# An attention and two-MLP kernel: SyncE's queue in the hand-written opening order, and preparations in nine steps

## The chip, the cores and the metric

The kernel runs on one NeuronCore of a Trainium2 chip. The metric is the device time of one execution in microseconds (us), as a median of several executions.

## The reference, cut to what matters

Chunked attention (chunks of 64 rows, 8 heads) feeds an MLP with squared ReLU, which feeds a gated MLP. Everything is float32.

```python
scores = scale * q_c @ k_c.T            # q, k, v: 8 x 8 x 576 x 64, chunks of 64
attn = exp(scores - max); attn /= sum(attn)
x = (attn @ v_c) as 4608 x 512
x = relu(x @ w_in) ** 2 @ w_out         # w_in 512 x 2048
out = (silu(x @ w_gate) * (x @ w_val)) @ w_out2
```

## The kernel before, in words

The 4608 tokens are nine blocks of 512. A block is two units of 256 tokens; attention works by units, numbered 0 to 17. The matrix products work by sets: set 0 is block 0 alone, sets 1 to 4 are pairs of blocks. A pair is multiplied with a seven-product scheme over the two blocks and the two halves of the contraction, a single block with four products. Each float32 product is three TensorE matmuls over a high and a low part (`three`, lines 517 to 522), so one of the seven products of a weight tile is six matmuls of 128x512.

The phases run one after another: the opening (attention of units 0 to 9, preparation of the eight weight tiles of w_in, the products of sets 0 and 1 with them), then w_in for sets 2 to 4 with the attention of the later units beside it, then `down1` (w_out, block by block), then w_gate and w_val, then w_out2.

**The opening** (lines 863 to 914) is a string of step names. Each name is a letter code and one digit, and the string is executed from left to right while the program is traced; PE, ACT, DVE and POOL execute their instructions in that order (`ordered`, line 916). SyncE (SP) was not in that list: the framework's own scheduler decided when each of its DMA issues goes into SyncE's queue. A queue executes in order, so an issue that waits holds up those behind it. The codes, with their lines:

- Attention of unit u: `qk` loads q and k (364), `v` loads v (369), `s` 64 small score matmuls (380), `m` the row maximum on DVE (397), `b` subtracts it on DVE (403), `e` exponential on ACT (406), `u` row sums and reciprocal on DVE (412 to 415), `w` the normalisation on POOL (419). Units 0 to 5 turn the rows with PE (`t`, 438) and copy them out on ACT (`c`, 450). Units 6 to 9 turn them on DVE (`zt`, 457), copy the square blocks on ACT (`zc`, 467) and then move four 32-row pieces per unit with DMAs of 64 KB on SyncE (line 471, tile p<-z). `y` is 64 small matmuls with v (495), `o` copies the result into x on ACT (511).
- Preparation of weight tile k: `raw` loads two tiles (115), `d1` on ACT (130, 131), `d2` on DVE (135, 136), `i` on POOL (143), `j` on DVE (148), `q` four sums on DVE (240 to 243), `h` and `g` the high parts on ACT (158), `l` and `n` the low parts on DVE (161), `st` stores the tile to DRAM on SyncE (256). `ld` loads a stored tile again (266).
- Operands of a set: `xd`, `xs`, `ys` differences on DVE (551), `xh`, `ph`, `qh` high parts on ACT, `xl`, `pl`, `ql` low parts on DVE, for sets 0, 1 and 2.
- Products of set 0 with tile k: `S` and `R` (twelve matmuls each), evicted by `sa` and `sb` on ACT. Products of set 1: `A`, `E`, `B`, `C`, `F`, `D`, `J` (six matmuls each), with the copies `ra`, `ub`, `vf` and the evictions `cd`, `cs` on ACT (610, 727, 736) and `ca`, `cb`, `cj` on DVE (596). Finished tiles g are stored by ACT's queue (737).

Three pools matter. Tiles of 128x1024 share 31 slots (`big`), the W tiles share 5, and the PSUM has six single banks plus one double bank. The double bank takes the scores and, from unit 6 on, the result of `y`. A load whose slot is not free waits in SyncE's queue for the release.

**Down1.** `beside_down1` (1189 to 1204) advances the preparation of the twelve tiles of w_gate and w_val by two steps after each of the products (b, i), from b = 1 on; `Prep.steps` (258 to 262) cuts one preparation into seven steps. When the last preparation has allocated its W tile, the first three stored W tiles are loaded (`up2.begin`, line 1201, `ahead` 3).

Of the kernel before, what the change touches and what calls it, by code (L numbers as in the profile page):

```python
# [29 lines left out]
def attention_mlp_mlp_kernel(  # L30
# [29 lines left out]
    nc = tc.nc  # L60
# [136 lines left out]
    class Prep:  # L197
# [58 lines left out]
                nc.sync.dma_start(out=wdram[self.key], in_=flat(self.w))  # L256

        def steps(self):
            for group in ("raw", "d1", "d2 i", "j h", "q", "g", "l n st"):
                for step in group.split():  # L260
                    getattr(self, step)()
                yield
# [8 lines left out]
    n2 = nf2 // 2  # L271
# [59 lines left out]
    class Work:  # L331
# [5 lines left out]
        def add(self, steps):  # L337
            self.queue.append(steps)
# [16 lines left out]
    at, vs = {}, {}  # L355
# [97 lines left out]
    def attn_z(u):  # L453

        e, pt = at[u], duo("p")
        z = duo("z")
        nc.vector.transpose(
            out=z.rearrange("p y (g t) -> p g y t", t=SQ),
            in_=e.rearrange("p j (g y t) -> p (j g) y t", y=2, t=SQ),
        )  # L460
        at[u] = z, pt

    def attn_squares(u):

        z, pt = at[u]
        at[u] = pt
        nc.scalar.copy(out=pt, in_=z)
        for c in range(2):
            for x in range(2):
                src, dst = c * CH + x * SQ, c * CH + (1 - x) * SQ  # L470
                nc.sync.dma_start(out=pt[dst:dst + SQ, x, :], in_=z[src:src + SQ, 1 - x, :])

    def attn_turn(u):
        attn_z(u)
        attn_squares(u)

    def attn_values(u):
        pt, vt = at.pop(u), vs.pop(u)
        if u < EARLY:
            xps = [bank("xps0"), bank("xps1")]  # L480
        else:
            xps = banks2("xps")
            xps = [xps[:, c, :] for c in range(2)]
        at[u] = xps
        for a in range(pairs):
            for n in range(2):
                for c in range(2):
                    for j in range(2):
                        h, g = 2 * a + j, (j * 2 + n) * pairs + a
                        part = slice(c * CH, (c + 1) * CH)  # L490
                        if u < EARLY:
                            rhs = pt[part, j ^ c, (n * pairs + a) * CH:(n * pairs + a + 1) * CH]
                        else:
                            rhs = pt[part, :, g * SQ:(g + 1) * SQ]
                        nc.tensor.matmul(
                            out=xps[c][j * CH:(j + 1) * CH, (a * 2 + n) * CH:(a * 2 + n + 1) * CH],
                            lhsT=vt[part, n, h * CH:(h + 1) * CH],
                            rhs=rhs,
                            start=True,
                            stop=True,  # L500
                        )
# [280 lines left out]
    n1 = nf1 // 2  # L782

    keys1 = [("i", fp) for fp in range(n1)]
# [8 lines left out]
    def ordered(*engines):  # L793

        return tc.manual_schedule(engines=set(engines))

    ET = mybir.EngineType
# [56 lines left out]
    up1 = Products(keys1, moving1, 2, 2, lambda key: Squared)  # L854

    def x_of(n):
        up1.ops[n] = Operands(xraw, sets[n])
        return up1.ops[n]

    def x_sums(n):  # L860
        x_of(n).sums()

    OPENING = """
        qk0 s0 raw0 d10 qk1 m0 b0 raw1 d20 i0 e0 qk2 s1 m1 d11 u0 v3 b1 j0 s2 qk3 e1 u1 m2 w0 raw2
        t0 w1 b2 h0 v1 d21 s3 t1 v0 q0 i1 c0 qk4 e2 y0 qk5 m3 u2 d12 b3 c1 s4 d22 w2 y1 m4 e3 t2 b4
        o0 v4 i2 u3 o1 e4 s5 c2 v2 w3 u4 m5 w4 xh1 y2 b5 xh2 t3 e5 c3 raw3 o2 xl2 t4 y3 c4 g0 u5 w5
        o3 l0 ph1 xl1 n0 t5 xd4 y4 v5 xh4 S0 j1 c5 raw4 y5 xl4 o4 qk6 h1 q1 pl1 g1 R0 o5 l1 n1 xs5
        sa0 sb0 xs6 xs7 ph6 ph2 A0 ra0 S1 pl6 R1 B0 pl2 ph7 ph5 j2 ub0 h2 pl7 q2 sa1 C0 s6 pl5 F0 l2
        d13 xs4 g2 n2 d23 A1 E0 ra1 B1 d14 sb1 ph4 S2 ca0 i3 C1 sa2 R2 j3 vf0 pl4 ph3 ub1 D0 cb0 sb2
        q3 pl3 h3 F1 st1 vf1 d24 raw5 l3 E1 A2 g3 n3 D1 ca1 i4 cb1 j4 ra2 cd0 B2 cd1 m6 J0 q4 C2 J1  # L870
        ub2 d15 cj1 d25 F2 g4 cj0 cs0 S3 A3 E2 ra3 sa3 h4 n4 i5 cs1 raw6 j5 vf2 B3 R3 ca2 cb2 ub3 C3
        d16 J2 F3 q5 l4 E3 d26 sb3 i6 D2 j6 h5 A4 vf3 cd2 ra4 ca3 D3 g5 B4 cb3 h6 ub4 J3 cj2 cs2 C4
        q6 raw7 g6 n5 l5 n6 b6 E4 ca4 cj3 cd3 F4 S4 d17 d27 vf4 A5 sa4 R4 D4 qk7 e6 ra5 i7 B5 j7 cb4
        l6 sb4 ub5 s7 C5 cs3 m7 st4 J4 F5 cd4 b7 u6 E5 A6 qk8 e7 ra6 q7 u7 qk9 s8 g7 cj4 B6 cs4 w7
        S5 m8 C6 n7 b8 h7 ca5 s9 sa5 ub6 w6 zt6 zc6 vf5 m9 l7 e8 zt7 zc7 F6 vf6 cb5 u8 R5 A7 v6 v7
        J5 b9 w8 ra7 cj5 B7 y6 S6 zt8 e9 o6 zc8 y7 sa6 o7 v8 st5 u9 D5 E6 y8 v9 cd5 w9 zt9 zc9 R6
        ca6 ub7 o8 sb5 C7 y9 S7 sb6 F7 R7 cb6 ca7 o9 J6 ys5 cs5 ys6 qh5 ys4 E7 sa7 D6 ys7 qh6 qh1
        ql1 sb7 ql5 vf7 cb7 st7 st2 ql6 qh2 cd6 qh7 qh4 ql2 ql4 ql7 qh3 cj6 ql3 ld1 cs6
    """

    def opening():

        jobs = {}

        def operands(n):
            return up1.ops[n] if n in up1.ops else x_of(n)

        def job(k, n=1):
            if (n, k) not in jobs:
                kind, late = ((Single, ()), (Pair, (1,)))[n]  # L890
                jobs[n, k] = kind(combos[keys1[k]], up1.ops[n], Squared(sets[n], k, late))
                jobs[n, k].use = (n, keys1[k])
            return jobs[n, k]

        steps = {
            "qk": attn_qk, "v": attn_v, "s": attn_products, "m": attn_max, "b": attn_less, "e": attn_exp,
            "u": attn_sums, "w": attn_normed, "t": attn_turn_pe, "c": attn_turned, "y": attn_values, "o": attn_out,
            "zt": attn_z, "zc": attn_squares, "ld": lambda m: up1.ask(up1.place[2, keys1[m]]),
        }
        for step in ("raw", "d1", "d2", "i", "j", "h", "q", "l", "g", "n", "st"):  # L900
            steps[step] = lambda k, step=step: getattr(preps[k], step)()
        for n, names in enumerate((("xd", "xh", "xl"), ("xs", "ph", "pl"), ("ys", "qh", "ql"))):
            for name, what in zip(names, ("sum", "high", "low")):
                steps[name] = lambda i, n=n, what=what: getattr(operands(n), what)(i)
        for name, what, i in (("S", "tile", 0), ("sa", "out", 0), ("R", "tile", 1), ("sb", "out", 1)):
            steps[name] = lambda k, what=what, i=i: getattr(job(k, 0), what)(i)
        parts = "A m1 ra k1 E m5 B m6 ub k6 C m2 ca k2 F m7 vf k7 cb o7 D m4 cd o4 J m3 cj o3".split()
        for name, what in zip(parts[::2], parts[1::2]):
            steps[name] = lambda k, what=what: getattr(job(k), what)()
        steps["cs"] = lambda k: job(k).take.square(1)  # L910
        for step in OPENING.split():
            steps[step[:-1]](int(step[-1]))
        jobs[1, n1 - 1].take.late = ()
        return jobs[1, n1 - 1]

    with ordered(ET.PE, ET.Activation, ET.DVE, ET.Pool):
        make_identity(nc, ident)
        up1.prev = opening()

# [187 lines left out]
    def attention_step(n, t):  # L1107

        if n < len(sets):
            units = [b * upb + x for b in sets[n] for x in range(upb)]  # L1110
            for what in ("out", "turn", "scores", "qk"):
                for u, when in zip(units, WHEN[what]):
                    if when == t:
                        if what == "out":
                            attn_values(u)
                            attn_out(u)
                        elif what == "turn":
                            attn_v(u)
                            attn_turn(u)
                        elif what == "scores":  # L1120
                            attn_scores(u)
                        else:
                            attn_qk(u)
# [193 lines left out]
```

## Time and profile before

| | us |
|---|---|
| median of 3 runs | 1645.68 |
| lowest, highest | 1643.70, 1648.36 |
| the profiled execution | 1643.45 |
| its span, first to last instruction | 1641.7 |
| PE busy | 1597.1 |

The profiled execution's own time is 1.75 us more than its span. PE is the tensor engine's matmul queue, PEld its weight loads, DVE the vector engine, ACT the scalar engine, POOL the GpSimd engine, SP SyncE; a q after a name is that engine's issue queue. A matmul's length in a row overlaps with its neighbours' (they are pipelined), so matmuls are counted by the distance of their starts. A bracket at the end of a row is the engine's idle time before it and what ended it; "issue" there means that the profile shows no releaser.

### The profile page before, as it was taken

Reading aid. Unit: us, or ns where it says so; the run is one execution under the profiler, and the core shown is the slowest. Engines: PE = TensorE matmul, PEld = TensorE weight load, DVE = VectorE, ACT = ScalarE, POOL = GpSimd, SP = SyncE. Lnnn points to the kernel's source line nnn. Section 1 sums busy time; section 2 is a strip of 40 time slices with the busy share of each in tenths; the row PEclk is TensorE's granted clock in tenths of the full one; section 3 lists DMA queues with packets and bytes.
Section 4 is the critical chain, followed back from the end, with each engine's and each line's share of the span. In section 5 each row is a group of like instructions: output and inputs, shape, how many; then the busy total and the mean of one; then the engine's idle time right before and its main releaser. Section 6 shows DMA issues by size and latency. Waiting matters only on the chain.

```text
span 1641.7 us, 23545 instructions
## 1 busy us (share of the span) xinstructions
PE 1597.1 (97%) x9408; PEld 1316.8 (80%) x9408; DVE 1017.7 (62%) x1248; ACT 760.5 (46%) x1069; POOL 150.4 (9%) x118
## 2 busy tenths in 40 slices
PE   5998999999999999999999999999999999999998
PEld 4787778888888888878888888888887787888886
DVE  7987465654487655553303556547458895887894
ACT  5875656666664443333211434334336553434441
POOL 4122030201131111100000000000000210000000
PEclk9999999999999999999999999999999999999999
DMA  8467697879767766774329676577668999564342
GB/s 321 181 250 245 227 338 266 295 252 341 265 229 256 267 246 256 256 285 157 116 67 388 217 282 230 194 256 244 216 246 299 366 393 408 211 205 132 101 140 52
DMA packets 136575, 397.92 MB, mean 242 GB/s; under 512 B 47760, under 2 KB 56976, under 8 KB 125584
## 3 DMA queue, kind: packets, MB, share of 16 engines
q1 hardware_dynamic: 118416, 345.02, 59.2%
q10 hardware_dynamic: 14592, 38.80, 6.3%
q0 software_dynamic: 3456, 12.58, 2.4%
q8 instruction: 74, 1.21, 0.3%
q14 instruction: 37, 0.30, 0.1%
HBM read 269.75 MB, written 123.47 MB: 240 GB/s over the span
## 4 chain that ended last, share of the span: by engine, by line
PE 52%; issue 6%; DMA 4%; DVE 2%; POOL 1%; SPq 0%; ACT 0%; POOLq 0%; DVEq 0%; ACTq 0%
PE px L520 8%; PE px L521 8%; PE px L522 8%; PE pz L520 4%; PE pz L521 4%; PE pz L522 4%; PE py L520 4%; PE py L521 4%; PE py L522 4%; DMA graw<-g 2%; PE acc L520 2%; PE acc L521 2%; PE acc L522 2%; DMA raw<-in_w_out_dram 1%; POOL m L143 1%
## 5 line engine op out<-in xcount | busy, mean ns | idle before, releaser
L520 PE MATMUL px<-hi,W 128*128 128x512 f32 x640 | 251.3, 393 | 1.9 <-ACT u L610 1.9
L521 PE MATMUL px<-hi,W 128*128 128x512 f32 x640 | 249.4, 390 | 0.0
L522 PE MATMUL px<-lo,W 128*128 128x512 f32 x640 | 249.4, 390 | 0.0
L143 POOL TENSOR_TENSOR m<-m,raw 128x512 int32<-128x512 int32 x68 | 97.2, 1446 | 1013.0 <-ACT r L610 552.5
L610 ACT COPY u<-px 128x512 f32<-128x512 f32 x160 | 92.6, 579 | 156.0 <-PE px L522 154.1
L520 PE MATMUL acc<-hi,w 128*128 128x512 f32 x416 | 162.3, 390 | 0.0
L521 PE MATMUL acc<-hi,w 128*128 128x512 f32 x416 | 162.1, 390 | 0.0
L522 PE MATMUL acc<-lo,w 128*128 128x512 f32 x416 | 161.6, 389 | 0.0
L161 DVE TENSOR_TENSOR lo<-graw,hi 128x1024 fp32r<-128x1024 f32 x72 | 92.2, 1281 | 83.8 <-ACT hi L158 51.1
L520 PEld LDWEIGHTS px<-hi,W 128*128 128x128 f32 x640 | 120.2, 188 | 29.9 <-ACT u L610 3.4
L158 ACT CAST hi<-h 128x1024 fp32r<-128x1024 f32 x93 | 95.6, 1053 | 96.5 <-PE py L521 16.3
L522 PEld LDWEIGHTS px<-lo,W 128*128 128x128 f32 x640 | 120.2, 188 | 25.0
L757 DVE TENSOR_TENSOR g<-g,sig 128x1024 f32<-128x1024 f32 x54 | 65.9, 1221 | 119.2 <-ACT sig L756 119.2
L521 PEld LDWEIGHTS px<-hi,W 128*128 128x128 f32 x640 | 120.2, 188 | 24.2
L520 PE MATMUL py<-hi,W 128*128 128x512 f32 x320 | 127.4, 398 | 0.4 <-DMA W<-wv 0.4
L520 PE MATMUL pz<-hi,W 128*128 128x512 f32 x320 | 124.9, 390 | 1.4 <-DVE g L593 1.4
L521 PE MATMUL py<-hi,W 128*128 128x512 f32 x320 | 125.7, 393 | 0.0
L522 PE MATMUL py<-lo,W 128*128 128x512 f32 x320 | 125.5, 392 | 0.0
L521 PE MATMUL pz<-hi,W 128*128 128x512 f32 x320 | 124.7, 390 | 0.0
L522 PE MATMUL pz<-lo,W 128*128 128x512 f32 x320 | 124.6, 389 | 0.0
L158 ACT CAST hi<-graw 128x1024 fp32r<-128x1024 f32 x72 | 75.5, 1049 | 88.7 <-DVE lo L161 36.7
L161 DVE TENSOR_TENSOR lo<-h,hi 128x1024 fp32r<-128x1024 f32 x93 | 110.2, 1212 | 4.5 <-issue 2.2
(125 smaller groups left out, 3055.1 us busy)
## 6 DMA issues: line engine op xcount, KB each, us to landing
W<-wv SPq DMA_DIRECT2D x30, 1792.0 KB, 9.0
g<-g ACTq DMA_DIRECT2D x72, 512.0 KB, 5.5
graw<-g SPq DMA_DIRECT2D x72, 512.0 KB, 4.4
W<-wg SPq DMA_DIRECT2D x20, 1792.0 KB, 8.3
h<-g SPq DMA_DIRECT2D x54, 512.0 KB, 8.2
h<-h SPq DMA_DIRECT2D x54, 512.0 KB, 6.2
W<-wi SPq DMA_DIRECT2D x15, 1792.0 KB, 10.0
raw<-in_w_out_dram SPq DMA_DIRECT2D x28, 512.0 KB, 8.2
```

Of the source, the lines that this page charges most:

```text
L143: nc.gpsimd.tensor_tensor(out=mi[:, t, :], in0=mi[:, t, :], in1=word(raw, 0, I32), op=ALU.add)
L158: nc.scalar.copy(out=hi, in_=src)
L161: nc.vector.tensor_tensor(out=lo, in0=src, in1=hi, op=ALU.subtract)
L520: nc.tensor.matmul(out=ps, lhsT=lh, rhs=rh, start=first, stop=False, skip_group_check=on)
L521: nc.tensor.matmul(out=ps, lhsT=ll, rhs=rh, start=False, stop=False, skip_group_check=on)
L522: nc.tensor.matmul(out=ps, lhsT=lh, rhs=rl, start=False, stop=last, skip_group_check=on)
L610: nc.scalar.copy(out=r, in_=self.x)
L757: nc.vector.tensor_tensor(out=g[j], in0=g[j], in1=s, op=ALU.mult)
```

## The change

SP joins the engines whose order is written out, until the end of the first pair. The moves of a unit's normed rows become a step of their own, `zd`, which the string places apart from `zc`. The string itself is another one: the same 396 steps and the four `zd`, in another order on every engine. One preparation of `Prep.steps` has nine steps in place of seven.

```diff
--- before.py
+++ after.py
@@ -256,7 +256,7 @@
                 nc.sync.dma_start(out=wdram[self.key], in_=flat(self.w))
 
         def steps(self):
-            for group in ("raw", "d1", "d2 i", "j h", "q", "g", "l n st"):
+            for group in ("raw", "d1", "d2 i", "j", "h", "q", "g", "l", "n st"):
                 for step in group.split():
                     getattr(self, step)()
                 yield
@@ -463,8 +463,12 @@
     def attn_squares(u):
 
         z, pt = at[u]
+        nc.scalar.copy(out=pt, in_=z)
+
+    def attn_moves(u):
+
+        z, pt = at[u]
         at[u] = pt
-        nc.scalar.copy(out=pt, in_=z)
         for c in range(2):
             for x in range(2):
                 src, dst = c * CH + x * SQ, c * CH + (1 - x) * SQ
@@ -473,6 +477,7 @@
     def attn_turn(u):
         attn_z(u)
         attn_squares(u)
+        attn_moves(u)
 
     def attn_values(u):
         pt, vt = at.pop(u), vs.pop(u)
@@ -861,21 +866,21 @@
         x_of(n).sums()
 
     OPENING = """
-        qk0 s0 raw0 d10 qk1 m0 b0 raw1 d20 i0 e0 qk2 s1 m1 d11 u0 v3 b1 j0 s2 qk3 e1 u1 m2 w0 raw2
-        t0 w1 b2 h0 v1 d21 s3 t1 v0 q0 i1 c0 qk4 e2 y0 qk5 m3 u2 d12 b3 c1 s4 d22 w2 y1 m4 e3 t2 b4
-        o0 v4 i2 u3 o1 e4 s5 c2 v2 w3 u4 m5 w4 xh1 y2 b5 xh2 t3 e5 c3 raw3 o2 xl2 t4 y3 c4 g0 u5 w5
-        o3 l0 ph1 xl1 n0 t5 xd4 y4 v5 xh4 S0 j1 c5 raw4 y5 xl4 o4 qk6 h1 q1 pl1 g1 R0 o5 l1 n1 xs5
-        sa0 sb0 xs6 xs7 ph6 ph2 A0 ra0 S1 pl6 R1 B0 pl2 ph7 ph5 j2 ub0 h2 pl7 q2 sa1 C0 s6 pl5 F0 l2
-        d13 xs4 g2 n2 d23 A1 E0 ra1 B1 d14 sb1 ph4 S2 ca0 i3 C1 sa2 R2 j3 vf0 pl4 ph3 ub1 D0 cb0 sb2
-        q3 pl3 h3 F1 st1 vf1 d24 raw5 l3 E1 A2 g3 n3 D1 ca1 i4 cb1 j4 ra2 cd0 B2 cd1 m6 J0 q4 C2 J1
-        ub2 d15 cj1 d25 F2 g4 cj0 cs0 S3 A3 E2 ra3 sa3 h4 n4 i5 cs1 raw6 j5 vf2 B3 R3 ca2 cb2 ub3 C3
-        d16 J2 F3 q5 l4 E3 d26 sb3 i6 D2 j6 h5 A4 vf3 cd2 ra4 ca3 D3 g5 B4 cb3 h6 ub4 J3 cj2 cs2 C4
-        q6 raw7 g6 n5 l5 n6 b6 E4 ca4 cj3 cd3 F4 S4 d17 d27 vf4 A5 sa4 R4 D4 qk7 e6 ra5 i7 B5 j7 cb4
-        l6 sb4 ub5 s7 C5 cs3 m7 st4 J4 F5 cd4 b7 u6 E5 A6 qk8 e7 ra6 q7 u7 qk9 s8 g7 cj4 B6 cs4 w7
-        S5 m8 C6 n7 b8 h7 ca5 s9 sa5 ub6 w6 zt6 zc6 vf5 m9 l7 e8 zt7 zc7 F6 vf6 cb5 u8 R5 A7 v6 v7
-        J5 b9 w8 ra7 cj5 B7 y6 S6 zt8 e9 o6 zc8 y7 sa6 o7 v8 st5 u9 D5 E6 y8 v9 cd5 w9 zt9 zc9 R6
-        ca6 ub7 o8 sb5 C7 y9 S7 sb6 F7 R7 cb6 ca7 o9 J6 ys5 cs5 ys6 qh5 ys4 E7 sa7 D6 ys7 qh6 qh1
-        ql1 sb7 ql5 vf7 cb7 st7 st2 ql6 qh2 cd6 qh7 qh4 ql2 ql4 ql7 qh3 cj6 ql3 ld1 cs6
+        qk0 s0 m0 raw0 d10 b0 qk1 e0 s1 d20 v1 u0 qk2 raw1 i0 m1 j0 b1 qk3 e1 v0 q0 w0 u1 w1 s2 m2
+        b2 qk4 d11 h0 raw2 d21 e2 u2 qk5 t0 s3 c0 t1 m3 b3 i1 v2 j1 y0 s4 g0 c1 y1 e3 w2 v3 o0 u3 m4
+        t2 w3 d12 b4 e4 c2 s5 d22 u4 i2 m5 o1 xh1 b5 xh2 e5 w4 xl2 v5 u5 t3 h1 w5 xl1 c3 y2 v4 t4 y3
+        c4 o2 o3 n0 l0 xd4 y4 t5 ph1 pl1 o4 S0 raw3 c5 A0 raw4 xh4 y5 q1 xl4 g1 d13 n1 ph2 l1 j2 q2
+        o5 h2 R0 S1 g2 st1 R1 ra0 sa0 sb0 l2 n2 xs5 xs6 S2 sa1 ph6 xs7 R2 sb1 pl6 pl2 ph7 B0 pl7 C0
+        ph5 pl5 qk6 ub0 sa2 F0 d23 A1 ca0 vf0 E0 cb0 ra1 B1 sb2 C1 ub1 i3 F1 xs4 ph3 j3 ph4 vf1 pl3
+        pl4 st2 A2 ca1 ra2 d14 h3 s6 E1 B2 q3 D0 J0 cb1 J1 raw5 g3 C2 d24 D1 l3 cd0 ub2 d15 cd1 n3
+        F2 cj1 raw6 cj0 A3 i4 j4 ra3 d25 vf2 cs0 q4 E2 h4 cs1 B3 g4 ub3 C3 D2 m6 E3 ca2 F3 d16 i5 S3
+        l4 j5 n4 qk7 ca3 d26 h5 vf3 cb2 cb3 i6 cd2 R3 j6 b6 sa3 J2 h6 sb3 J3 cj2 s7 A4 ra4 q5 st4 D3
+        B4 g5 S4 l5 raw7 e6 E4 q6 n5 cj3 l6 cs2 cd3 qk8 cs3 ub4 u6 g6 w6 C4 F4 n6 m7 A5 b7 ra5 qk9
+        d17 sa4 R4 e7 s8 ca4 d27 vf4 B5 zt6 C5 D4 zc6 ub5 u7 i7 sb4 S5 m8 j7 F5 A6 b8 cb4 zd6 sa5 w7
+        e8 ra6 s9 zt7 vf5 J4 D5 m9 cd4 v6 h7 v7 B6 q7 l7 R5 C6 zc7 zd7 ub6 cj4 b9 g7 n7 u8 v9 e9 u9
+        F6 A7 v8 sb5 E5 y6 w8 w9 ra7 ca5 B7 vf6 cb5 cd5 zt8 C7 zc8 o6 ub7 zt9 zc9 zd8 E6 J5 zd9 y7
+        o7 cj5 cs4 S6 y8 ca7 ca6 F7 o8 cb6 D6 y9 o9 st7 R6 ys5 cd6 ys6 ys7 J6 S7 sa6 ys4 E7 vf7 sb6
+        qh1 st5 qh5 qh2 ql1 ql5 sa7 qh6 R7 ql2 cb7 qh7 ql6 cj6 qh3 cs5 ql7 ql3 cs6 qh4 ql4 sb7 ld1
     """
 
     def opening():
@@ -895,7 +900,8 @@
         steps = {
             "qk": attn_qk, "v": attn_v, "s": attn_products, "m": attn_max, "b": attn_less, "e": attn_exp,
             "u": attn_sums, "w": attn_normed, "t": attn_turn_pe, "c": attn_turned, "y": attn_values, "o": attn_out,
-            "zt": attn_z, "zc": attn_squares, "ld": lambda m: up1.ask(up1.place[2, keys1[m]]),
+            "zt": attn_z, "zc": attn_squares, "zd": attn_moves,
+            "ld": lambda m: up1.ask(up1.place[2, keys1[m]]),
         }
         for step in ("raw", "d1", "d2", "i", "j", "h", "q", "l", "g", "n", "st"):
             steps[step] = lambda k, step=step: getattr(preps[k], step)()
@@ -913,7 +919,7 @@
         jobs[1, n1 - 1].take.late = ()
         return jobs[1, n1 - 1]
 
-    with ordered(ET.PE, ET.Activation, ET.DVE, ET.Pool):
+    with ordered(ET.PE, ET.Activation, ET.DVE, ET.Pool, ET.SP):
         make_identity(nc, ident)
         up1.prev = opening()
```

## Rows read from the trace of the kernel before

**Rows 1.** The page, part 1: busy time by engine, share of the span, instructions

```profile
PE 1597.1 (97%) x9408; PEld 1316.8 (80%) x9408; DVE 1017.7 (62%) x1248; ACT 760.5 (46%) x1069; POOL 150.4 (9%) x118
```

**Rows 2.** Stretches: length, busy time of PE, PEld, DVE, ACT, POOL, granted clock, DMA share, GB/s

```profile
0.00:53.00 53.00, 30.08 (x1090) 28.44 (x1091) 42.64 (x49) 30.07 (x52) 20.95 (x20) 0.94 0.81 294
53.00:156.00 103.00, 102.95 (x745) 84.09 (x743) 88.72 (x115) 74.90 (x109) 20.25 (x13) 1.00 0.61 228
156.00:186.00 30.00, 21.68 (x310) 17.47 (x309) 7.49 (x10) 13.61 (x28) 1.90 (x1) 0.83 0.68 231
```

**Rows 3.** Timeline of PE, 152 to 185 us: start, length, line, tile, count [idle before]

```profile
152.02 0.39 PE L520 MATMUL px<-hi,W 128*128 128x512 f32 x1
...
155.88 0.39 PE L522 MATMUL px<-lo,W 128*128 128x512 f32 x1
161.13 2.10 PE L495 MATMUL xps<-p,v 64*64 64x64 f32 x64 [4.86 <-issue]
163.15 0.79 PE L520 MATMUL py<-hi,W 128*128 128x512 f32 x1
...
167.99 1.16 PE L495 MATMUL xps<-p,v 64*64 64x64 f32 x64
...
181.11 2.22 PE L495 MATMUL xps<-p,v 64*64 64x64 f32 x64 [3.45 <-DMA p<-z]
...
184.53 0.39 PE L520 MATMUL py<-hi,W 128*128 128x512 f32 x1
```

**Rows 4.** Timeline of SyncE's queue, 152 to 178 us: issues, first start and length

```profile
152.75 1.44 SPq L369 DMA_DIRECT2D v<-in_v_dram  x2
154.24 13.59 SPq L471 DMA_DIRECT2D p<-z  x8
167.93 1.07 SPq L369 DMA_DIRECT2D v<-in_v_dram  x2
...
173.98 3.48 SPq L471 DMA_DIRECT2D p<-z  x4
```

**Rows 5.** Issue to landing: tile p, 140 to 190 us; tile v, until 190 us

```profile
DMA to landing us min/median/max: 1.9/3.7/8.8
...
DMA to landing us min/median/max: 3.9/10.0/12.1
```

**Rows 6.** Timeline of DVE and ACT, 154 to 174 us

```profile
154.94 0.69 DVE L596 CUSTOM_DVE_ANT_0 g<-pz,u 128x512 f32<-128x512 f32 x1 [0.47 <-PE pz L522]
...
163.26 1.20 ACT L511 COPY x<-xps 128x256 f32<-128x256 f32 x4 [7.63 <-PE xps L495]
163.32 1.25 DVE L457 STREAM_TRANSPOSE z<-e 128x1024 f32<-128x1024 f32 x1 [4.93 <-DMA p<-z]
...
172.91 1.05 ACT L467 COPY p<-z 128x1024 f32<-128x1024 f32 x1 [0.47 <-DVE g L596]
```

**Rows 7.** Timeline of all engines, 13 to 53 us

```profile
13.21 1.22 DVE L397 TENSOR_REDUCE mx<-s 128x16 f32<-128x1024 f32 x1 [1.44 <-PE s L380]
...
46.22 2.34 POOL L419 TENSOR_TENSOR e<-e,rec 128x1024 f32<-128x1024 f32 x1 [3.35 <-DVE rec L415]
46.72 2.92 DVE L161 TENSOR_TENSOR lo<-x,hi 128x1024 fp32r<-128x1024 f32 x1
...
51.83 1.28 DVE L148 SCALAR_TENSOR_TENSOR m<-raw,m 128x512 int32<-128x512 int32 x2
...
52.47 0.50 PE L520 MATMUL py<-hi,W 128*128 128x512 f32 x1
```

**Rows 8.** Waits of SyncE's queue, 60 to 120 us: total, times, longest

```profile
SPq L115 <- DMA g<-g: 7.2, 2, 6.6
```

**Rows 9.** The longest wait of PE after 300 us, and its stretch

```profile
PE accs L520 <- ACT hi L158: 2.0, 1, 2.0
...
730.00:740.00 10.00, 7.80 (x28) 5.50 (x27) 3.71 (x4) 4.21 (x4) 0.00 (x0) 0.83 0.79 288
```

**Rows 10.** Timeline of SyncE's queue, 706 to 725 us: one of three such issues

```profile
711.59 0.42 SPq L266 DMA_DIRECT2D W<-wv  x1
```

## The prediction

> **What bounds the kernel now.** Start with the page's busy times. TensorE (PE) is busy for 1597.1 us [rows 1] of a span of 1641.7, so no order of any queue can win more than the 44.6 us in which PE stands idle, plus what its slow clock costs. The next view is the table of stretches, which shows where those idle times lie. In the first 53 us PE is busy for 30.1, so 22.9 are idle, while DVE works for 42.6. From 53 to 156 us PE is never short of work, and from 156 to 186 it is idle for 8.3 us again, at a granted clock of 0.83 on average [rows 2]. After 300 us its longest single wait is 2.0 us [rows 9]. The change touches the two idle places and nothing between 186 and 440.
>
> The timeline of PE shows what the second place is. The last of the products ends at 156.1 us (a start at 155.88 and one matmul). PE then waits 4.86 us for `y6`, and 3.45 us ahead of `y9` [rows 3]. After each wait the records show matmuls at the lower clock level, 1.2 GHz, until work had run for some us. SyncE's queue says why. v6 and v7 were issued only at 152.75, eight moves then occupy the queue until 167.8, v8 and v9 follow at 167.93, and the moves of unit 9 at 173.98 [rows 4]. A v load takes 10.0 us to land in the median, a move 3.7 [rows 5]. So `y6` waited for SyncE (v6 or the moves of unit 6, the row names neither), and `y9` for the moves of unit 9, which waited for ACT's `zc9` at 172.91 [rows 6].
>
> **The change, part by part.**
>
> The second idle place. A matmul's pitch is (155.88 - 152.02) / 17 = 0.227 us, so a product of six takes 1.36 us and one of twelve (`S`, `R`) 2.72; a `y` at the full clock takes 1.16 [rows 3]. What can go is 4.86 + 3.45 = 8.31 us of idle time, and the slow stretches behind it. From 161.13 these are 2.10 - 1.16 = 0.94 for `y6` and (167.99 - 163.15) - 12 x 0.227 = 2.12 for the twelve matmuls after it. From 181.11 they are 184.53 - 181.11 - 1.16 - 3 x 0.227 = 1.58 [rows 3]. Together it is 12.95 us.
>
> Does the new order remove it? It puts J4 D5 B6 R5 C6 F6 A7 E5 between `s9` and `y6`, which is 7 x 1.36 + 2.72 = 12.2 us of work, where the old one had F6 R5 A7 J5 B7, 8.2 us. v6 follows `zd6` in SyncE's queue. Counting tiles against the 31 slots, it needs at the latest the slots of q9 and k9, which `s9` frees. So even from there it has 12.2 us against a landing of 10.0 in the median and 12.1 at most [rows 5], and `y6` is met. `zd6` needs `zc6`, which the string has some 20 us of PE work ahead of `y6`.
>
> The later units run closer. Up to `y6` the new order holds one product fewer than the old one had up to 156.1. With the first product `S0` at 51.2 (below), `y6` starts at 51.2 + (156.1 - 52.5) - 1.36 = 153.5. Then B7 C7 E6 J5 put `y7` at 160.1, S6 puts `y8` at 164.0, F7 and D6 put `y9` at 167.9. Against this stands unit 8: E5 ends at 153.5, `cb5` takes 0.69, `zt8` 1.25, `zc8` 1.05 [rows 6], so `zd8` can start at 156.5. Its last of four issues starts some 2.6 later (3.48 for four [rows 4]) and lands 3.7 after that, at 162.8; with the longest landing of 8.8 [rows 5], at 167.9. So `y8` has 1.2 us to spare, or is 3.9 late. For unit 9 ACT does `o6` (1.20 [rows 6]) and one half-size copy (about 0.6, half of `zc`) ahead of `zc9`, which is done by 159.4; the last move starts at 162.6 and lands at 166.3, or 171.4. `y9` has 1.6 to spare, or is 3.5 late, unless a late `y8` has moved it too. The worst is therefore 3.9 and a slow stretch as that behind `y9` now, 1.6: 5.5 us. I take half, 2.75, since both margins are small against the spread of the landings. The operands of set 2 follow `y9` by about 8 us, and 10.9 us of products (R6 J6 S7 E7 R7) stand ahead of their first use, so nothing new is late there.
>
> The first idle place. The new string sends the loads up to k1 in the old order, so the first score products stay where they are. On DVE, `u0` now stands ahead of `m1` and fills the 1.44 us in which DVE waited for the second score product; `j1` comes ahead of the last sums `u5` and adds 1.28. On PE, `y4` moves ahead of `t5`, which waits for POOL's normalisation until 48.6 (46.22 + 2.34), so `S0` no longer stands behind `y4`: 1.16 less [rows 3, 7]. The sum is -1.3, which puts `S0` at 51.2 in place of 52.47. That `n0` now stands ahead of `l0` costs nothing as long as `xl1`, `n0`, `l0` on DVE (three instructions of 1.2 us or less, or 5.0 with `xl1` at the 2.92 it took beside POOL [rows 7]) stay within the 2.34 of the normalisation and the two to three us of `t5`, which come out near the same. Bounds: 3 us less, or 3 more if DVE is slowed beside POOL as `xl1` was.
>
> The middle, 53 to 156 us. SyncE's issues are now fixed: `st1` ahead of qk6, `st2` ahead of raw5, raw7 ahead of qk8. Each store waits for DVE's `n`, and every load behind it waits with it; behind raw7 stand `s8` and `s9`. By counting, DVE's parts are ready ahead of PE throughout, nearest at `B0` (2.9 us), and the six banks never bind. The slots are nearly all taken at raw5 and raw6. Nothing hides a late slot fully: the longest wait of that kind is 6.6 us, a raw load that waited for ACT's store of g [rows 8]. I take 0, since qk7, raw7 and qk8 have two or more slots to spare, and keep 0 to 6.6.
>
> Down1. Nine steps spread the same instructions over 54 pairs of steps in place of 42, so DVE and ACT do less per product, but PE has no wait on them now. The last preparation allocates its W tile at the 52nd call in place of the 41st, 11 x 24 x 0.227 = 60 us later, and three W loads are issued at once there, now at 711.6 [rows 10]. They delay g tiles, and PE lost 2.2 us idle and (1 - 0.83) x 7.8 = 1.3 by the clock [rows 9]. I move this, at no gain: 0, with bounds of -3.5 (the burst finds more cover) and +3.5 (a second one).
>
> The sum: -12.95 - 1.3 + 2.75 = -11.5, against the profiled execution's 1643.45 it is 1632.0. The median of the runs is 2.2 above that execution, so the forecast is **1634.2 us**.
>
> **The rivals.**
> Landings stay slow. SyncE's order says when a transfer is issued, not when it lands: a move of 64 KB took up to 8.8 us beside others [rows 5]. With `zd8` at that end the sum is -14.2 + 5.5 = -8.7, **1637**. Against it: v6 and v7 no longer stand among the moves of units 6 and 7.
> The Trainium skill, DMA: Bandwidth & Descriptors, section "Issuing engines are not separate DMA queues", says that DMAs of all issuing engines run on the same 16 DMA engines and interleave. By that rule ACT's g stores would delay `zd8` whatever SyncE's order is, which gives this rival's 1637; the spread from 1.9 to 8.8 agrees with it.
>
> One new wait in the middle. A slot released by a g store holds raw6 or raw7 for 6.6 us [rows 8], `s7` or `s8` is late by it, and the clock falls as behind `y6` (0.94 + 2.12). -11.5 + 9.7 = -1.8: **1644**.
>
> The change does not do what it says. The scheduler may have had SyncE's queue in much this order already; if the moves still land when they did, only the front's 1.3 us are left: **1644.4**. Against it stands that `zc9` waited for ACT's order, which is new.
>
> Slower: the fixed queue holds up what stands behind it. Three waits of 6.6 us, at raw6 (`s7`), raw7 (`s8`) and v8 (`y8`), each with a slow stretch of 1.6 to 3.1: 19.8 + 7 = 26.8, less the 14.2: **1658**. It decides from the point where such waits pass 14.2 + 4.9 us. Against it: before, two such waits came to 7.2 us in total [rows 8].
>
> **How the numbers follow.** A measurement of this kernel can tell about 0.3%, 4.9 us, from no change. Chances: forecast 0.42 (1629 to 1637), slow landings 0.17, one new wait 0.18, no effect 0.10, slower 0.13. Faster by over 0.3% are the first two and a little of the third, 0.61; within it 0.26; slower 0.13. The range reaches from 1645.7 - 14.2 - 3.5 = 1628 to 1648, which takes in the cases of 1644 and leaves out the slower one and some of the edges.
>
> **What would show it.** Right: in the timeline of PE no idle time over 1 us between `S0` and `y8`; v6 issued by 143 us; the stretch of 156 to 186 us at a clock of 1.00; the opening's last product near 180 in place of 194. Wrong: a wait at `s7` or `s8` on a q or k load, raw loads held by g<-g in SyncE's waits, `y8` ended by DMA p<-z, a first 53 us with less PE work than 30.1, or a longer wait of accs in down1 near 780 us.

## The result, and the profile after

| | before | after |
|---|---|---|
| median, us | 1646.62 (4 runs, 1643.70 to 1648.36) | 1624.49 (4 runs, 1624.17 to 1625.45) |
| the profiled execution, us | 1643.45 | 1624.17 |
| its span, us | 1641.7 | 1622.4 |

The ratio is 0.9868, with a 95% interval of 0.9851 to 0.9885: the changed kernel is faster by 22.1 us, nearly twice what was forecast, and its time lies below the range.

Lines of the kernel after have moved: L520 to L522 are now L525 to L527, L495 is L500, L471 is L475, L593 is L598, L610 is L615, and L467 is L466.

Page of the kernel after, part 1, which answers to [rows 1]:

```profile
PE 1590.1 (98%) x9408; PEld 1312.2 (81%) x9408; DVE 1014.0 (63%) x1248; ACT 759.4 (47%) x1069; POOL 149.2 (9%) x118
```

PE is busy for 7.0 us less with the same 9408 matmuls, so fewer of them ran at the lower clock level, and it is idle for 1622.4 - 1590.1 = 32.3 us in place of 44.6. The two make up the 19.3 us by which the spans differ.

Stretches of the kernel after, columns as in [rows 2]:

```profile
53.00:156.00 103.00, 103.00 (x803) 84.07 (x802) 87.81 (x117) 74.51 (x106) 21.52 (x14) 1.00 0.65 237
156.00:186.00 30.00, 30.00 (x308) 24.41 (x307) 17.17 (x18) 22.59 (x39) 4.45 (x6) 1.00 0.76 289
...
158.90:165.30 6.40, 6.40 (x88) 4.92 (x86) 2.48 (x4) 4.66 (x11) 0.00 (x0) 1.00 0.53 156
```

From 156 to 186 us PE is now never idle and the granted clock is 1.00 (21.68 us busy and 0.83 before). The same DMA engines moved more there, 289 GB/s in place of 231, but not while the moves of units 8 and 9 were on their way: that is the last row, with 156 GB/s.

Timeline of PE of the kernel after, answering to [rows 3]: the four `y` have no wait ahead of them and run in 1.16 us, the length of the full clock.

```profile
154.57 1.16 PE L500 MATMUL xps<-p,v 64*64 64x64 f32 x64
...
161.33 1.16 PE L500 MATMUL xps<-p,v 64*64 64x64 f32 x64
...
165.37 1.16 PE L500 MATMUL xps<-p,v 64*64 64x64 f32 x64
...
169.41 1.16 PE L500 MATMUL xps<-p,v 64*64 64x64 f32 x64
```

SyncE's queue of the kernel after, 139 to 190 us (start, length from the first issue of a group to the last, count):

```profile
139.62 2.28 SPq L369 DMA_DIRECT2D v<-in_v_dram  x2
146.00 2.41 SPq L475 DMA_DIRECT2D p<-z  x4
148.46 1.93 SPq L369 DMA_DIRECT2D v<-in_v_dram  x2
158.90 4.95 SPq L475 DMA_DIRECT2D p<-z  x8
163.89 1.08 SPq L256 DMA_DIRECT2D wi<-W  x2
177.43 11.40 SPq L266 DMA_DIRECT2D W<-wi  x2
```

And its landings: tile p from 125 to 190 us, then the four v loads from 139 to 151.

```profile
DMA to landing us min/median/max: 1.9/2.0/2.4
...
DMA to landing us min/median/max: 3.4/4.5/5.4
```

v6 is issued at 139.62 in place of 152.75. The store and the loads of W tiles, which in the kernel before came among the moves (a W load of 1792 KB stood at 170.74, ahead of unit 9's), now come behind all of them. The longest recorded landing of a move is 2.4 us in place of 8.8 [rows 5].

From the queue of the kernel before, three rows that [rows 4] do not show, and the landings of its moves, those issued from 149.19, from 154.24 and from 173.98:

```profile
149.19 2.82 SPq L471 DMA_DIRECT2D p<-z  x4
152.12 0.53 SPq L256 DMA_DIRECT2D wi<-W  x1
...
170.74 0.34 SPq L266 DMA_DIRECT2D W<-wi  x1
```

```profile
DMA to landing us min/median/max: 2.0/2.0/2.0
...
DMA to landing us min/median/max: 5.8/7.0/8.8
...
DMA to landing us min/median/max: 5.4/6.0/6.3
```

So unit 6's moves had gone out and landed by 153.5. The eight moves of [rows 4] are unit 7's, from 154.24 to 158.45, and unit 8's, from 165.42 on, which landed in 1.9 to 2.0 us; between them the queue stood still. v6 stood behind the store of a W tile, 1792 KB issued at 152.12, and took 8.2 us: it landed at 160.9, and `y6` started at 161.13.

Where the 19.3 us came from can be read off three marks of PE's timeline: `S0`, the first product of down1 (tile accs) and its last one. "Opening" is from `S0` to the first product of down1, so it holds the later sets of w_in too. The experiments below are in the table already; the median is from several runs, the middle columns from the profiled one. Each experiment was timed beside runs of the kernel before, whose median was 1643.9 to 1647.1 us there, so kernels of different rows are best compared by the ratio to it.

| kernel | v6 issued | opening | down1 | median | ratio |
|---|---|---|---|---|---|
| before | 152.75 | 388.0 | 402.4 | 1646.6 | |
| before, profiled again (e10) | 152.28 | 392.5 | 402.4 | 1647.0 | 0.9998 |
| after | 139.62 | 374.3 | 398.3 | 1624.5 | 0.9868 |
| after, seven steps (e1) | | 373.5 | 399.9 | 1624.5 | 0.9866 |
| after, moves inside zc (e5) | | 374.3 | 398.3 | 1623.8 | 0.9859 |
| after, both (e9) | 139.77 | 374.8 | 399.7 | 1625.8 | 0.9869 |
| after, SyncE free (e3) | 144.13 | 376.4 | 398.3 | 1626.4 | 0.9876 |
| after, W store and load ahead of moves (e8) | | 380.8 | 398.3 | 1630.1 | 0.9908 |
| before, nine steps (e2) | | 391.1 | 398.3 | 1642.3 | 0.9969 |
| before, SyncE ordered (e4b) | 157.37 | 382.5 | 398.3 | 1634.8 | 0.9937 |
| the same, v6 and v7 early (e11) | 141.44 | 375.3 | 402.2 | 1629.2 | 0.9892 |
| the same, nine steps (e12) | 140.84 | 375.8 | 398.3 | 1627.0 | 0.9895 |
| before, v by POOL's queue (e6) | 148.60 | 385.6 | 399.1 | 1641.0 | 0.9977 |
| before, one W load by ACT's queue (e7) | | 391.5 | 403.1 | 1645.8 | 0.9998 |

The opening gave 13.6 us, down1 4.2, `S0` 0.2 and what lies behind down1 1.2. The other 2.8 of the 22.1 are how the profiled runs lie to their medians: 3.2 below for before, 0.3 for after.

### The profile page after: what moved, and what is told of

Its sections match the earlier page's. It is cut to its first block, busy times and chain, and to the rows that moved or that the text cites. A ratio compares the mean times of both kernels' runs of the same rounds, so it can differ in the third digit from the quotient of the medians.

```text
span 1622.4 us, 23523 instructions
## 1 busy us (share of the span) xinstructions
PE 1590.1 (98%) x9408; PEld 1312.2 (81%) x9408; DVE 1014.0 (63%) x1248; ACT 759.4 (47%) x1069; POOL 149.2 (9%) x118
## 4 chain that ended last, share of the span: by engine, by line
PE 95%; DMA 2%; DVE 1%; ACT 1%; issue 1%; SPq 0%; POOL 0%; ACTq 0%; DVEq 0%; POOLq 0%
PE px L525 12%; PE px L527 11%; PE px L526 11%; PE acc L525 6%; PE acc L527 6%; PE acc L526 6%; PE pz L525 6%; PE pz L527 6%; PE pz L526 6%; PE py L525 6%; PE py L527 5%; PE py L526 5%; PE accs L525 2%; PE accs L527 2%; PE accs L526 2%; PE s L380 1%
## 5 line engine op out<-in xcount | busy, mean ns | idle before, releaser
L525 PE MATMUL px<-hi,W 128*128 128x512 f32 x640 | 251.0, 392 | 0.7 <-ACT u L615 0.7
L527 PE MATMUL px<-lo,W 128*128 128x512 f32 x640 | 249.2, 389 | 0.0
L615 ACT COPY u<-px 128x512 f32<-128x512 f32 x160 | 93.0, 581 | 157.9 <-PE px L527 154.8
L525 PE MATMUL acc<-hi,w 128*128 128x512 f32 x416 | 161.8, 389 | 0.0
L527 PE MATMUL acc<-lo,w 128*128 128x512 f32 x416 | 161.5, 389 | 0.0
L525 PEld LDWEIGHTS px<-hi,W 128*128 128x128 f32 x640 | 120.1, 188 | 27.9 <-ACT u L615 2.1
L527 PEld LDWEIGHTS px<-lo,W 128*128 128x128 f32 x640 | 120.1, 188 | 25.2
L525 PE MATMUL pz<-hi,W 128*128 128x512 f32 x320 | 125.0, 391 | 1.4 <-DVE g L598 1.4
L525 PE MATMUL py<-hi,W 128*128 128x512 f32 x320 | 125.9, 394 | 0.3 <-DMA W<-wv 0.3
L527 PE MATMUL py<-lo,W 128*128 128x512 f32 x320 | 124.7, 390 | 0.0
L527 PE MATMUL pz<-lo,W 128*128 128x512 f32 x320 | 124.5, 389 | 0.0
```

Of the source, the lines that this page charges most:

```text
L525: nc.tensor.matmul(out=ps, lhsT=lh, rhs=rh, start=first, stop=False, skip_group_check=on)
L527: nc.tensor.matmul(out=ps, lhsT=lh, rhs=rl, start=False, stop=last, skip_group_check=on)
L615: nc.scalar.copy(out=r, in_=self.x)
```

## The experiments

The theory at the start was that SyncE's explicit order carries the gain at the `y` products; the rival gave it to PE's new order.

**One part of the change undone at a time.** Seven steps again (e1):

```diff
-            for group in ("raw", "d1", "d2 i", "j", "h", "q", "g", "l", "n st"):
+            for group in ("raw", "d1", "d2 i", "j h", "q", "g", "l n st"):
```

> The changed kernel with seven steps per preparation again. Theory: the nine steps alone removed the wait of accs in down1 (2.2 us idle and 1.3 us by the clock), so it comes back here: about 3.5 us over the changed kernel's 1624.5, that is 1628.0, with a wait of 2 us of accs on ACT's hi near 710 us. Rival: that wait was a matter of how the opening had placed everything after it, and the new opening removed it: 1624.5, no wait of accs.

1624.45 us, ratio to before 0.9866 (0.9851 to 0.9880). The accs waits are 0.5 and 0.5 us, not the 2.0 of [rows 9], and down1 took 399.9 us. In the new kernel nine steps are worth 1.6 us of down1 in the profiles, and nothing that the medians can tell.

Nine steps alone in the kernel before (e2), the diff's first hunk and nothing else:

> The kernel before with nine steps per preparation and nothing else. Theory: 3.5 us under the kernel before, 1643.1 against 1646.6, and no wait of accs over 0.5 us. Rival (the opening did it): 1646.6, the wait is still there.

1642.27 us, ratio 0.9969 (0.9953 to 0.9985). Here the accs wait goes, and down1 takes 398.3 us in place of 402.4.

SyncE out of the explicit order (e3):

```diff
-    with ordered(ET.PE, ET.Activation, ET.DVE, ET.Pool, ET.SP):
+    with ordered(ET.PE, ET.Activation, ET.DVE, ET.Pool):
```

> The changed kernel, with SyncE taken out of the engines whose order is written out; string and steps stay. Theory (SyncE's order carries the gain at the y products): the v loads or the moves are issued late again, PE waits 2 to 8 us ahead of y6 to y9: 1628 to 1636. Rival (the new order of PE, with more products ahead of y6, carries it): within 2 us of 1624.5, no wait of xps over 1 us.

1626.39 us, ratio 0.9876 (0.9861 to 0.9890): 1.9 us above the kernel after. No `y` waits, so the rival held. With the new string the scheduler itself issued v6 at 144.13 and all the moves ahead of the W load (167.93).

The moves inside zc again (e5):

```diff
-            "zt": attn_z, "zc": attn_squares, "zd": attn_moves,
+            "zt": attn_z, "zc": lambda u: (attn_squares(u), attn_moves(u)), "zd": lambda u: None,
```

> The changed kernel with the four moves of a unit issued in the step zc again (zd does nothing), SyncE still ordered. Theory: the moves' place in SyncE's queue changes only where zc and zd stand apart (units 6 and 8; v8 and v9 keep their place), the moves wait no longer: 0 to 2 us over 1624.5. Rival (the separate step is what lets loads pass the moves): a wait of y6 or y8 of 3 us and its slow stretch, 1629.

1623.78 us, ratio 0.9859 (0.9845 to 0.9874), no `y` wait: a step of its own for the moves is worth nothing here.

e1 and e5 together (e9) ask whether the two small parts cover for each other:

> The kernel after with both small parts undone at once: the moves inside zc again, and seven steps in place of nine; the new string and SyncE's explicit order stay. Theory (the string and SyncE's order carry all of it; each small part alone measured nothing): within 2 us of the kernel after, 1623 to 1626.5, down1 no longer than 400.5 us. Rival (the small parts cover for each other): 1628 or more, with a y wait or an accs wait above 1.5 us.

1625.76 us, ratio 0.9869 (0.9852 to 0.9886). They don't, by more than the intervals. So the new string with an ordered SyncE carries the gain, and the string with SyncE left to the scheduler most of it (e3).

**The other way round: SyncE's order on the old string** (e4b). The stores are put right behind the step that they wait for, since a fixed queue can't reach past them:

```diff
- l1 n1 xs5
+ l1 n1 st1 xs5
...
-    with ordered(ET.PE, ET.Activation, ET.DVE, ET.Pool):
+    with ordered(ET.PE, ET.Activation, ET.DVE, ET.Pool, ET.SP):
```

> The kernel before with SyncE in the explicit order, on the old string; the stores st1, st2, st4, st5, st7 stand right behind the later of n and l, since the old string has them where a fixed SyncE order cannot wait for them. Moves stay inside zc. Theory (PE's order carries the gain, SyncE's order about 2 us): y6 still stands behind only F6 R5 A7 J5 B7 after s9 and v6 still behind the moves of units 6 and 7 in SyncE's queue, so y6 and y9 wait 3 to 5 us each and the time is 1640 to 1650. Rival (the free SyncE order was what held the v loads up): y6's wait below 1 us, 1632 to 1638.

From here on the theory is that of e3's rival, PE's order. 1634.83 us, ratio 0.9937 (0.9915 to 0.9960). The theory misses; the rival has the time right and its reason wrong, since `y6` still waits. PE's waits from 156 to 200 us (total, times, longest):

```profile
PE xps L495 <- DMA v<-in_v_dram: 5.8, 1, 5.8
```

SyncE's queue in the same run:

```profile
152.56 4.70 SPq L471 DMA_DIRECT2D p<-z  x4
157.37 1.07 SPq L369 DMA_DIRECT2D v<-in_v_dram  x2
...
174.09 2.77 SPq L471 DMA_DIRECT2D p<-z  x4
176.96 0.53 SPq L266 DMA_DIRECT2D W<-wi  x1
```

`y6` waited as the theory had it, for v6, which now stood behind the moves of units 6 and 7 and the W store. But `y9`'s wait is gone: the W load of 170.74 in the kernel before now comes at 176.96, behind unit 9's moves. So there were two faults in the old queue, v6 late and behind a W store, and a W load ahead of moves, and this order mends the second. That theory, which gave SyncE's order 2 us, fell.

The new one: what counts is the place of v6 in SyncE's queue, and PE's order matters only where it, or the scheduler, sets that place. e11 moves nothing but two loads in e4b's string:

```diff
- s9 sa5 ub6 w6 zt6 zc6
+ s9 sa5 ub6 v6 v7 w6 zt6 zc6
...
- u8 R5 A7 v6 v7 J5 b9
+ u8 R5 A7 J5 b9
```

> The old string with SyncE in the explicit order (as in the run of that name, 1634.8 us), and the loads v6 and v7 moved ahead of w6, so that they stand ahead of the moves of units 6 and 7 in SyncE's queue; PE's order is the old one. Theory (what held y6 was only v6's place in SyncE's queue): v6 is issued near 148 us in place of 157.4 and lands by 154, the move of unit 6 lands by about 157, so y6 waits 1 us or less in place of 5.8 and the time is 1626 to 1630. Rival (PE's order is needed too, since only 8.2 us of products stand between s9 and y6): v6 gets its slot only behind s9, lands after 158, y6 waits 3 us or more, 1631 to 1636.

1629.20 us, ratio 0.9892 (0.9873 to 0.9911). SyncE's queue, and below it PE's waits from 440 to 850 us:

```profile
141.44 5.47 SPq L369 DMA_DIRECT2D v<-in_v_dram  x2
149.46 2.52 SPq L471 DMA_DIRECT2D p<-z  x4
152.08 0.52 SPq L256 DMA_DIRECT2D wi<-W  x1
...
PE accs L520 <- ACT hi L158: 2.1, 1, 2.1
```

`y6` starts at 156.46 without a wait, still behind only F6 R5 A7 J5 B7. The slot of v6 was free before `s9`, at 141.44, which the rival had not allowed for. The opening takes 375.3 us with PE's old order, 374.3 with the new one. What is left is down1's wait (and 1.3 us ahead of `y8`, for v8), so e12 adds nine steps:

> The run with v6 and v7 ahead of w6 on the old string (1629.2 us, down1 402.2 us from its first to its last product, with accs waits of 2.6 us), with nine steps in place of seven. Theory (nine steps take the accs wait away wherever it appears): down1 takes 398.3 us, no accs wait, 1624 to 1627, so that the old string with SyncE's order, two loads moved and nine steps comes within 2 us of the kernel after. Rival (the accs wait of that run came from something else): 1628 to 1630, an accs wait of over 1 us stays.

1626.98 us, ratio 0.9895 (0.9877 to 0.9914). The accs waits are gone and down1 takes 398.3 us, as expected, but behind down1 this execution took 1.5 us more (PE waited 2.0 us for ACT's copies of u, 0.7 in e11), the median is 2.5 us above the kernel after and not within the 2 that were expected, and the ratios of e11 and e12 can't be told apart.

**What the moves waited for.** e6 takes the v loads of units 6 to 9 out of the old kernel's SyncE queue:

```diff
-        loader(u).dma_start(out=vt, in_=v[2 * u:2 * u + 2].rearrange("n p c -> p n c"))
+        (nc.sync if u < EARLY else nc.gpsimd).dma_start(out=vt, in_=v[2 * u:2 * u + 2].rearrange("n p c -> p n c"))
```

> The kernel before with the v loads of units 6 to 9 issued by POOL's queue instead of SyncE's. Theory (y6 waited for v6, which was issued at 152.75 and landed 8.2 us later): v6 is issued by POOL near 144 us and lands by 152, so y6 loses its wait of 4.86 us or keeps less than 1; y9's wait stays at 2 to 4. Time 1638 to 1643. Rival (y6 waited for the moves of unit 6): y6's wait stays at 4 to 6 us, the time within 2 us of the kernel before.

1641.02 us, ratio 0.9977 (0.9966 to 0.9989). `y6` starts at 156.57 and waits for nothing, which [rows 3] could not say: it was v6, as its landing at 160.9 had it. The moves of unit 7, still behind the W store, took 6.6 to 7.2 us to land though no v load stood ahead of them in SyncE's queue. `y9` waits longer than before, in PE's waits of this run:

```profile
PE xps L495 <- DMA p<-z: 6.4, 3, 4.9
```

The W load now stands at 166.09 and the moves of unit 9, from 169.39 on, take 7.6 to 7.7 us to land, the two of them whose landing was recorded.

e7 takes that W load out of SyncE's queue instead:

```diff
-            "zt": attn_z, "zc": attn_squares, "ld": lambda m: up1.ask(up1.place[2, keys1[m]]),
+            "zt": attn_z, "zc": attn_squares, "ld": lambda m: load_combo(keys1[m], nc.scalar),
```

(`load_combo` takes the queue as an argument.)

> The kernel before with the load of the next W tile at the end of the string (issued by SyncE at 170.74, 1792 KB, ahead of the moves of unit 9) issued by ACT's queue behind its last step of the string instead. Theory (the moves of unit 9 landed in 5.4 to 6.3 us only because that load stood ahead of them): they land in 2.0 to 2.5 us and y9's wait falls from 3.45 to below 1; time 1640 to 1645. Rival (the moves were late because zc9 was): y9's wait stays at 3 to 4, landings 5 to 6.

1645.81 us, ratio 0.9998 (0.9985 to 1.0012). The moves of unit 9 landed in 2.0 to 3.2 us and `y9` waited for nothing, though `zc9` was no earlier (172.3 against 172.91), so the rival is out, and with it the prediction's reason for `y9`'s wait. The gain was lost on the next step. PE's waits from 156 to 300 us:

```profile
PE px L520 <- DMA W<-wi: 7.5, 1, 7.5
PE xps L495 <- issue: 4.8, 1, 4.8
```

In ACT's queue the load went out only at 194.54, and the first product of the next set stood for it. It may be neither ahead of the moves nor much behind them.

e8 puts such transfers ahead of the moves in the kernel after:

```diff
- zt9 zc9 zd8 E6 J5 zd9 y7
+ zt9 zc9 st5 zd8 E6 J5 ld1 zd9 y7
...
- qh1 st5 qh5
+ qh1 qh5
...
- ql4 sb7 ld1
+ ql4 sb7
```

> The kernel after with the store st5 put ahead of zd8 and the W load ld1 ahead of zd9, so that SyncE's queue has about 1 MB and 1.8 MB ahead of the two groups of moves. Theory (moves land in 2.0 us in the kernel after only because no large transfer stands ahead of them): the moves of units 8 and 9 land in 5 to 9 us and y8 or y9 waits 2 to 6 us, clock below 1.00 in the stretch 156 to 186; time 1627 to 1633. Rival (landings depend on what all queues move, not on what stands ahead in this one): landings stay at 2 to 2.5, no wait, 1624 to 1626.

1630.13 us, ratio 0.9908 (0.9883 to 0.9932): 5.6 us lost by the medians, 6.6 by the ratios. (The store is 1792 KB too, not 1 MB.) SyncE's queue, the landings of unit 8's and of unit 9's moves, of the first of unit 9's alone, that of the W load between them, and PE's wait:

```profile
150.97 0.47 SPq L256 DMA_DIRECT2D wi<-W  x1
158.47 2.84 SPq L475 DMA_DIRECT2D p<-z  x4
163.17 0.34 SPq L266 DMA_DIRECT2D W<-wi  x1
163.56 2.40 SPq L475 DMA_DIRECT2D p<-z  x4
...
DMA to landing us min/median/max: 4.1/5.0/5.8
...
DMA to landing us min/median/max: 9.1/9.7/9.9
...
DMA to landing us min/median/max: 9.8/9.8/9.8
...
DMA to landing us min/median/max: 9.6/9.6/9.6
...
PE xps L500 <- DMA p<-z: 4.2, 1, 4.2
```

The first move behind the W load landed at 163.56 + 9.8 = 173.4, the load itself at 163.17 + 9.6 = 172.8. The run has more bytes on their way at that moment as well as another order in the queue, so it does not tell the theory from its rival. A later unit of the kernel before, shown below under the slow landings, has the rival partly right. Behind that wait `y9` ran at the lower clock level, 2.39 us in place of 1.16.

**The scatter of the kernel before** (e10, unchanged):

> The kernel before, unchanged, profiled a second time. Theory (its runs scatter because the waits at y6, y9 and in down1 depend on when transfers land): the waits of y6 and y9 and the accs wait differ from the first profile's 4.86, 3.45 and 2.0 us by up to 2 us each, and explain the difference of the two profiled executions; the span from S0 to the start of the w_out products differs by over 1 us. Rival (the scatter is elsewhere): these waits repeat within 0.3 us.

1647.44 us in this execution, 4.0 more than in the first. PE's waits from 150 to 200 us:

```profile
PE xps L495 <- issue: 5.1, 1, 5.1
PE xps L495 <- DMA g<-g: 4.9, 1, 4.9
PE xps L495 <- DMA v<-in_v_dram: 1.1, 1, 1.1
PE xps L495 <- DMA p<-z: 0.6, 1, 0.6
```

These are 11.7 us against 8.3 in [rows 3], and the opening took 4.5 us longer, down1 the same 402.4. The W load was issued at 169.39 and landed 11.5 us later, and the moves behind it 8.8 to 8.9 after their issue. Of the 3.4 us, 2.1 are at `y9`; `y6`'s wait repeats within 0.3 us. So between these two executions most of the difference is in waits that the change removes. That all the scatter is there is not shown: e1 has no `y` wait either, and its four runs span 4.1 us.

## Why the prediction was wrong in its size

The mechanism and the sign were right, the size was not: 1634.2 forecast, 1624.5 measured. Two terms failed, the +2.75 for stalls at `y8` and `y9`, which measured 0, and the 0 for down1, which measured -4.2. The 9.7 us between are 2.4 up to down1 (2.75 of the stalls and 0.7 of the opening that no term had, less 1.1 that `S0` did not give), 4.2 in down1, 1.2 behind it, and 1.9 in the offset of the median.

- **The second idle place, -12.95.** Right. v6 went out at 139.62, before the 143 that was asked for, the stretch of 156 to 186 us has clock 1.00, and from `S0` to down1 13.6 us went. That PE's string had to cover v6 with 12.2 us of work was not needed: e11 covers it with the old 8.2. Two readings behind the term were wrong all the same. The eight moves did not occupy the queue until 167.8, it stood still from 158.45 to 165.42; and what made `y9` wait was the landing behind the W load of 170.74, not `zc9` (e7).
- **The stalls at `y8` and `y9`, +2.75.** This step failed. It took half of a bound of 5.5 that came from the longest landing, 8.8 us [rows 5], as if that were a chance spread. It is not: a landing goes by what is in flight ahead of the move. The move that took 8.8 had the W store and two v loads of 512 KB ahead of it, issued 0.8 to 2.1 us earlier; the four from 149.19 on had none of these and landed in 2.0 us, which landings read group by group would have told. In the new queue nothing large stands close ahead of `zd8` and `zd9`, and their moves landed in 1.9 to 2.1. `zd8` did start 2.4 us later than forecast (158.90 against 156.5), and still its last move, issued at 160.73, landed by about 162.7 (an estimate from the three before it, its own landing was not recorded), for a `y8` at 165.37. With e8's queue the moves took 4.1 to 9.9 us and `y9` waited 4.2.
- **Landings stay slow, 1637.** They did not, but the rule behind the rival holds. The rule of the Trainium skill that was weighed there, DMA: Bandwidth & Descriptors, section "Issuing engines are not separate DMA queues", says that all DMAs share 16 engines and interleave whoever issues them. The runs agree that another queue can delay a move: with v6 issued by POOL, one us ahead (e6), the first of four moves took 4.0 us to land (the only one recorded), against 2.0 in the kernel before. A later unit of the kernel before shows it alone, with nothing in flight from SyncE's own queue and three loads of 512 KB from POOL's. Issues, and the landings of the moves:

```profile
300.33 0.74 POOL L364 DMA_DIRECT2D q<-in_q_dram  x1
301.07 0.72 POOL L364 DMA_DIRECT2D k<-in_k_dram  x1
301.79 0.72 POOL L369 DMA_DIRECT2D v<-in_v_dram  x1
302.76 2.42 SPq L471 DMA_DIRECT2D p<-z  x4
...
DMA to landing us min/median/max: 6.2/6.6/7.8
```

  What the rival had wrong is how much would be in flight: when the moves of units 8 and 9 went out in the kernel after, the only large transfer on its way was one g store of 512 KB, issued at 157.40 and landed at 160.0. No run has a W load in another queue beside the moves, so how the cost of own and other queues compares is open.
- **The first idle place, -1.3.** Measured -0.2. The 1.28 us of `j1` ahead of `u5` came, the normalisation ahead of `t5` started 1.3 later, and the 1.44 filled by `u0` were lost again: DVE waited 0.79, 1.13 and 2.32 us for score products. Timeline of POOL and PE:

```profile
47.51 2.67 POOL L419 TENSOR_TENSOR e<-e,rec 128x1024 f32<-128x1024 f32 x1 [5.24 <-DVE rec L415]
...
50.23 2.08 PE L438 MATMUL et<-ident,e 64*64 64x64 f32 x64 [0.90 <-POOL e L419]
52.24 0.50 PE L525 MATMUL py<-hi,W 128*128 128x512 f32 x1
```

  Over the runs `S0` lay between 51.5 and 53.8 us, so one profile can't settle a term of this size.
- **The middle, 0 with up to 6.6.** 0 was right, and the sign that was to show it wrong was badly chosen. Raw loads did wait for g<-g, longer than in [rows 8]. Waits of SyncE's queue, 53 to 130 us, of the kernel after:

```profile
SPq L115 <- PE s L380: 15.0, 1, 15.0
...
SPq L115 <- DMA g<-g: 11.1, 2, 9.5
```

  PE had no wait from 53 to 156 us all the same. A queue's wait is a price only where what stands behind it is due, so the rival of 1644 and the slower one of 1658 had their waits and not their cost.
- **Down1, 0 with -3.5 to +3.5.** It gave 4.2, past its bound. The eight executions with seven steps took 402.4, 402.4, 403.1, 402.2, 399.9, 399.7, 399.1 and 398.3 us, the six with nine all 398.3. Of the 4.2, only 1.6 belongs to the nine steps in the new kernel; 2.5 had come with the new opening alone (399.9 in e1), which the term did not have at all. The step that failed is taking 0, the middle of two bounds, where [rows 9] showed a loss in the very place that was changed. The tile loaded behind the burst of W loads landed after 18.9 to 19.4 us with seven steps, whether down1 lost time or not (19.4 before, 18.9 in e4b, which lost nothing), and after 15.1 to 16.5 where recorded with nine. What the loss goes with is when the burst comes, counted from down1's first product:

  | run | e4b | e6 | e9 | e1 | before, e10 | e7 | e11 | the six with nine steps |
  |---|---|---|---|---|---|---|---|---|
  | first W load, us into down1 | 268.3 | 269.3 | 269.7 | 270.0 | 271.1 | 271.8 | 272.1 | 315.6 to 318.6 |
  | down1, us | 398.3 | 399.1 | 399.7 | 399.9 | 402.4 | 403.1 | 402.2 | 398.3 |

  So an opening that shifts the burst by 3 us goes with the whole loss, and the nine steps moved it by 45 us, not by the 60 of the prediction. No run moved the burst alone, so this cause is read from the traces and not shown.
- **The offset.** The forecast took over the 2.2 us by which before's median lies above its profiled run. The kernel after lies 0.3 above its own, and its four runs span 1.3 us instead of 4.7. That the waits took their scatter with them is likely, not shown: without `y` waits the runs of e3 and e5 span 0.7 and 1.0 us, but those of e1 4.1 and of e9 2.9.

The low end of the range, 1645.7 - 14.2 - 3.5 = 1628, lies 3.5 us too high: 1.9 is this offset, 1.2 came behind down1, 0.7 is down1 past its bound, and the opening with `S0` gave 0.4 less than 14.2.

PE's waits behind 300 us are what is left there, the first of them as before and the accs waits gone:

```profile
PE pz L525 <- DVE g L598: 1.4, 1, 1.4
PE px L525 <- ACT u L615: 0.7, 1, 0.7
PE py L525 <- DMA W<-wv: 0.3, 1, 0.3
```

Of the two larger parts either is nearly enough: the new string with SyncE left to the scheduler comes to a ratio of 0.9876, the old string with an ordered SyncE, two loads moved and nine steps to 0.9895, against 0.9868, and the intervals overlap. None of the versions beats the kernel after by more than the intervals.

## What to carry to other kernels

Read a small urgent transfer by what is in flight ahead of it, in its own queue and in the others, not by when it is issued. Here the 64 KB moves of units 6 to 9 landed in 2.0 us with nothing large ahead and in 3 to 10 behind a W store or W load of 1792 KB, and a later unit's in 6 to 8 behind three loads of 512 KB in another queue. Place large loads behind the urgent ones, but no further than their own use (e7). Of a landing's spread, ask which transfers make up its slow end before it is taken for chance.

## What was not expected of the hardware

A move behind a W load in SyncE's queue landed just behind that load and not before it: 173.4 against 172.8 in e8, in e10 at 172.63 + 8.9 = 181.5 against 169.39 + 11.5 = 180.9, and in the kernel before at 180.2 against 179.6, 0.6 us each time. Behind three loads of POOL's queue it was the same, 309.3 against 309.1 for the last of these. What is ahead is thus paid in landing time as well as in issue time.
